# A fused attention and two-layer mixture-of-experts kernel: token gates turned earlier, sums of squares on GpSimd, router parts spread

## The chip, the cores and the metric

The kernel runs on one core of a Trainium2 chip. The metric is device time in microseconds (us), the median of several runs. Engines: TensorE (PE), VectorE (DVE), ScalarE (ACT), GpSimd (POOL), and SyncE (SP), which here only issues DMAs.

## What is computed

Sigmoid attention over 4 batches of 448 tokens, then two mixture-of-experts layers over all 1792 tokens of width 768, with 8 experts of 1024 hidden features each. Everything is fp32.

```python
def _moe2_ref(x, expert_emb, tau, w1, w2):
    xn = x / (np.linalg.norm(x, axis=-1, keepdims=True) + 1e-06)
    en = expert_emb / (np.linalg.norm(expert_emb, axis=-1, keepdims=True) + 1e-06)
    logits = xn @ en.T / tau
    expert_idx = np.argmax(logits, axis=1)
    ...
    gate_w = probs[np.arange(N), expert_idx]
    for e in range(E):
        mask = expert_idx == e
        h = np.maximum(x[mask] @ w1[e], 0.0)
        out[mask] = gate_w[mask, None] * (h @ w2[e])
```

Layer 1 (`_moe_ref`) is of the same form, with a linear router, a skip test, and `x + y` as its result. The change lies in layer 2 and in the sum of squares that its router's norm needs.

## The kernel before

**Layout.** `xT` holds x transposed: 128 features on the partitions, 6 chunks of features (`ND`), 1792 tokens along the row. A batch is 448 columns.

**A dense block.** Almost all tokens of a batch go to one expert, so that expert runs over the whole batch (`dense`, L801 on) and the few other tokens are handled by an `Item` of up to 64 tokens. Each fp32 factor is split in a high and a low part (ScalarE writes `h`, `hh`, `xs`; VectorE writes the remainders `l`, `hl`), and every product is three matmuls (L795 to L797). For f in 0 to 7 a block computes `h(f)`: 18 matmuls from `xs` into one of two PSUM banks, evicted by ScalarE (`hh`, L815) and then VectorE (`hl`, L816); and `y(f - 1)`: 18 matmuls from `hh`, `hl` into six PSUM tiles `YS`. The order on TensorE is h(0), h(1), y(0), h(2), y(1), ..., h(7), y(6), y(7).

**Sub-steps.** Other work is hung between these groups by a table of numbers: `sub(2f)` is called after h(f), `sub(2f + 1)` after y(f - 1). So sub-step 6 lies between h(3) and y(2), and 14 between h(7) and y(6). At each even sub-step the weights of the next unit are split first (`units2`, L785 and L786), then come the steps of the table. Every engine runs its own instructions in this program order.

**Banks.** `bank()` hands out the two banks in turn to whoever asks: h(f), and each small product of a router, of a gate or of an item. An item's `places` (L942) flips the turn once more, and so gets the bank that was handed out last. A matmul into a bank waits until the earlier contents have been read.

**Blocks of layer 2.** Batches j = 0, 1, 2 are stored by `finish`: VectorE transposes `YS` (L1347), GpSimd multiplies by the tokens' gates `gt` (L1349), and SP issues the stores at sub-step 2 of the next block. `gate_tokens` (L1328) makes `gt` at sub-step 14: four small VectorE operations (L357 to L361, L1333), one matmul pair (L1338), a copy (L1340). Batch 3 ends by `finish_last`, with an `Item` whose `places`, gather and gate come at sub-steps 5, 5 and 7; the gather is 64 GpSimd copies (L954) that feed L977 at sub-step 13.

**Routers of layer 2.** For batches 1 to 3 the table `ROUTED` gives the sub-steps of eight parts: raw copy and squares (ScalarE, L1075 and L1081), `squares_sum` (L1084), s1 (L245 matmuls, the last of them with the sum `G`), s2 (L262 transposes, then VectorE up to the one-hot `OH`, L283), s3 (L288, L289, then a VectorE chain), `scaled_logits`, and `gates` (L340 to L348: two ScalarE operations, then five of VectorE). Batches 1 and 2 are routed in block 0, batch 3 in block 1, batch 0 in layer 1.

Of the kernel before, what the change touches and what calls it, by code (L numbers as in the profile page):

```python
# [10 lines left out]
F32 = mybir.dt.float32  # L11
# [3 lines left out]
ALU = mybir.AluOpType  # L15
AX = mybir.AxisListType
# [5 lines left out]
def sigmoid_attention_moe_moe_kernel(  # L22
# [15 lines left out]
    nc = tc.nc  # L38
# [3 lines left out]
    P = 112  # L42
    C = S // P
    NP = H // 2
    ND = DM // 128
# [3 lines left out]
    NK = S // 32  # L49
# [8 lines left out]
    sm = ctx.enter_context(tc.tile_pool(name="sm", bufs=2))  # L58
# [7 lines left out]
    def bank(name):  # L66
        if not BANKS:
            return psA.tile([128, 512], F32, tag="psA", name=name)
        turn[0] ^= 1
        return BANKS[turn[0]]  # L70

    def spare():
        turn[1] ^= 1
        return XG[turn[1]]
# [13 lines left out]
    K = {}  # L88
# [263 lines left out]
    def dense_gate(R, b, g=None):  # L352
        t = sm.tile([P, C, NE], F32, tag="dgt", name="dgt")
        if g is None:
            g = sm.tile([P, C], F32, tag="dg", name="dg")
        one = lambda x, pat: x.rearrange(pat)
        nc.vector.tensor_mul(  # L357
            t, one(R.OH[:, ds(b, 1)], "p o e c -> p (o c) e"), R.PRIM[:P, ds(b, 1)].to_broadcast([P, C, NE])
        )
        nc.vector.reduce_sum(g, t, axis=AX.X)  # L360
        nc.vector.tensor_mul(g, g, one(K["gr"][R.m][:, ds(b, 1), :, 0], "p o c -> p (o c)"))  # L361
        return g
# [147 lines left out]
    def merge(*steps):  # L510

        out = {}
        for t in steps:
            for k in sorted(t):
                f = t[k]
                out.setdefault(k, []).extend(f if isinstance(f, list) else [f])
        return out

    def schedule(at, prep, slots):

        assert len(slots) == len(prep)
        return merge(at, *({k: f} for k, f in zip(slots, prep)))
# [164 lines left out]
    R1, R2 = Route(0), Route(1)  # L687
# [80 lines left out]
    SEL = wp.tile([128, 4 * 128], F32, tag="sel", name="sel")  # L768
# [76 lines left out]
    def at_subs(ks, fs):  # L845
        return merge(*({k: f} for k, f in zip(ks, fs)))
# [36 lines left out]
    class Item:  # L883
# [139 lines left out]
        def ready(self, k0):  # L1023

            prep = [self.places, self.gather(0, TL), self.gate]
            at = merge({k0: [self.regs, self.select]}, {5: [lambda: self.first(0)]}, {
                7: [lambda: self.first(1)], 9: [lambda: self.first(2)], 11: [lambda: self.first(3)],
                13: [self.h(0)], 14: [self.hT(0), lambda: self.second(0, 1)],
                15: [self.h(1), lambda: self.second(2, 3)],
            })  # L1030
            return at, prep
# [41 lines left out]
    def raw(b):  # L1073
        for p in range(ND):
            nc.scalar.activation(XR[:, p], batch_cols(p, b), AF.Copy)  # L1075

    SQ = ROW[:, : ND * S].rearrange("p (c s) -> p c s", s=S)
# [3 lines left out]
            nc.scalar.activation(SQ[:, p], XR[:, p], AF.Square)  # L1081

    def squares_sum():
        nc.vector.reduce_sum(K["G"], SQ.rearrange("p c s -> p s c"), axis=AX.X)  # L1084

    def batch_of(j):
        return nc.values_load(K["pb"][0:1, 8 + j : 9 + j], engines=XENG, min_val=0, max_val=B - 1)

    def expert_of(j):
        return nc.values_load(R2.I[0:1, j : j + 1], engines=[ENG.SP], min_val=0, max_val=NE - 1)  # L1090

    def route2_steps(j, xs):

        box = {}

        def halves(p):
            def f():
                if p == 0:
                    box["b"] = batch_of(j)
                    box["p"] = split_batch(xs, box["b"])  # L1100
                for g in box["p"][p : p + 2]:
                    g()

            return f

        return (
            [halves(p) for p in range(0, ND, 2)]
            + [lambda: raw(batch_of(j)), squares, squares_sum]
            + route_stages(R2, j, lambda c: XR[:, c])
            + [scaled_logits, lambda: gates(R2, j, j + 1)()]  # L1110
        )
# [8 lines left out]
    def next_dense(j):  # L1120

        box = {}
        xs = XST[(j + 1) % 2]

        def start():
            box["b"], box["e"] = rest_regs(j)
            load1(w1, box["e"], 0)
            load2(w2, box["e"], 0)
            gate_cols(R1, box["b"])

        def rows():
            gate_rows(bank("ps_G"))
            box["p"] = split_gated(xs, box["b"])
            for p in range(2):
                box["p"](p)

        def last():
            load_unit(w1, w2, box["e"], 1)
            for f in split_unit(0)[:3]:
                f()  # L1140

        return {
            8: start, 10: rows, 11: lambda: [box["p"](p) for p in (2, 3)], 12: lambda: [box["p"](p) for p in (4, 5, 6)], 13: last,
            14: lambda: [f() for f in split_unit(0)[3:]],
        }
# [115 lines left out]
    def item_steps(R, at):  # L1261
        return at_subs(at, item_list(R))
# [21 lines left out]
    with tc.If(na > 0) as cmp:  # L1284
# [4 lines left out]
        with tc.If(NB["n"] > 0) as cmp2:  # L1289
            steps = merge(next_dense(0), item_steps(R1, (10, 12, 15)), {12: lambda: raw(batch_of(0)), 15: squares})  # L1290
# [4 lines left out]
        with cmp2.Else():  # L1295
            steps = merge(rest2(), item_steps(R1, (9, 11, 12)))
# [30 lines left out]

    def gate_tokens(j, box):  # L1328

        g = dense_gate(R2, j)  # L1330
        a = spare()[:P, :128]
        four = [P, 4, C, 8]
        nc.vector.tensor_tensor(  # L1333
            a.rearrange("p (g c r) -> p g c r", g=4, r=8), g.unsqueeze(1).unsqueeze(3).to_broadcast(four),
            K["seg"][:P].unsqueeze(1).unsqueeze(1).to_broadcast(four), op=ALU.mult,
        )
        ps = bank("ps_gt")
        nc.tensor.matmul(ps[:, :NK], lhsT=a, rhs=K["off"][:P], start=True, stop=True)  # L1338
        t = box["gt"] = sm.tile([128, NK], F32, tag="gtt", name="gtt", bufs=1)
        nc.vector.tensor_copy(t, ps[:, :NK])  # L1340

    def finish(j, b, gt):

# [18 lines left out]
    def finish_last(j, b, it=None):  # L1362
# [56 lines left out]

    pend, STORES = None, []  # L1420
    ROUTED = {
        0: [(1, (1, 2, 2, 5, 6, 8, 9, 10)), (2, (7, 7, 9, 11, 12, 13, 15, 15))],
        1: [(3, (3, 7, 7, 9, 10, 11, 13, 15))],
    }
    assert B == 4
    for j in range(B):
        box = {"e": e}
        last = j == B - 1
        if last:
            todo = {}  # L1430
        else:
            todo = at_subs((3, 5, 7), route2_steps(j + 1, XST[(j + 1) % 2])[:3])
            for n, at in ROUTED.get(j, ()):
                todo = merge(todo, at_subs(at, route2_steps(n, None)[3:]))
            todo = merge(todo, {14: lambda j=j, box=box: gate_tokens(j, box)})
        if j == 0:
            load_unit(v1, v2, e, 1)
            halves()
            for f in split_unit(0, FIRST_RAW)[3:]:
                f()  # L1440
            todo = merge({-0.5: lambda: spread(item_b())}, todo)
        if j == B - 2:
            todo = merge(todo, item_steps(R2, (9, 11, 13)))
        if pend:
            todo = merge({2: pend}, todo)

        def units2(k):
            u, r = k // 4, k % 4
            if r == 0 and u + 2 < NU:
                load_unit(v1, v2, box["e"], u + 2)  # L1450
            if k == 10 and not last:
                box["n"] = expert_of(j + 1)
                load_unit(v1, v2, box["n"], 0)
            if (u + 1 < NU or not last) and r % 2 == 0:
                for f in split_unit((u + 1) % NU)[:3] if r == 0 else split_unit((u + 1) % NU)[3:]:
                    f()
            if k == 12 and not last:
                load_unit(v1, v2, box["n"], 1)

        xs = XST[j % 2]  # L1460
        if not last:
            dense(xs, beside(units2, todo))
            pend = finish(j, b, box["gt"])
            b, e = nc.values_load(K["pb"][0:1, 9 + j : 10 + j], engines=[ENG.SP], min_val=0, max_val=B - 1), box["n"]
            continue
        with tc.If(count(R2) > 0) as cmp:
            it = Item(1, 0)
            at, prep = it.ready(0)
            steps = schedule(merge(todo, at), prep, (5, 5, 7))
            dense(xs, beside(units2, steps), end=finish_last(j, b, it))  # L1470
            it.finish([None] * 3)
            info = mybir.DependencyInfo(mybir.DependencyClass.Sync, mybir.DependencyReason.DATA)
            tc.add_manual_dep(it.put().ins, STORES[0].ins.name, info, reason="the rows it lands on")
        with cmp.Else():
            STORES = []
            dense(xs, beside(units2, todo), end=finish_last(j, b))
# [36 lines left out]
```

## Time and profile before

| | |
|---|---|
| median of 3 runs | 586.06 us (585.79 to 587.38) |
| the profiled execution's own time | 585.59 us |
| its span | 583.7 us |
| busy: PE, DVE, ACT, POOL | 554.8, 303.8, 251.7, 60.5 us |
| mean granted TensorE clock | 0.984 |
| layer 2, blocks 0 to 3 start at | 290.4, 365.2, 433.5, 501.2 us |

A row of the timeline gives start, duration, engine, line, operation, output and input by name, and in brackets the idle time before it and what ended it. Matmuls are pipelined and their ends are modelled: within a run of them one starts every 0.20 us though each is shown with 0.36 us.

### The profile page before, as it was taken

The page shows a single profiled execution, that of the slowest core. Times are in us where ns is not written, and L with a number is a line of the kernel's source. Part 1 is how long each engine was busy: PE and PEld are TensorE (multiplying, and loading weights), DVE is VectorE, ACT ScalarE, POOL GpSimd, SP SyncE. Part 2 cuts the span into 40 slices and gives each one's busy share as a digit, 9 for nine tenths or more (in the row PEclk, how much of TensorE's full clock was granted, in tenths as well). Part 3 has the DMA queues.
Part 4 walks back from the last instruction along what each step waited for, and adds up shares of the span by engine and source line. Part 5 has one row for each costly group of instructions (what it writes and reads, how often), then busy time and mean ns, then how long its engine had stood idle before and what let it go on. Part 6 is the DMA issues. An engine that isn't in the chain of part 4 may idle for free.

```text
span 583.7 us, 10179 instructions
## 1 busy us (share of the span) xinstructions
PE 554.8 (95%) x3653; PEld 432.7 (74%) x3653; DVE 303.8 (52%) x775; ACT 251.7 (43%) x408; POOL 60.5 (10%) x165
## 2 busy tenths in 40 slices
PE   8999999999999999999899987999799997999995
PEld 5564645444698988998598876997789996989782
DVE  2725333456775796742288776456646432533221
ACT  5766766767722643322185511563205321222120
POOL 4010000000000001640000001200030000315300
PEclk9999999999999999999999997999989997999999
DMA  9877685746414133335470251382215633274163
GB/s 172 148 125 122 113 140 105 125 83 233 156 62 163 57 111 111 108 116 211 149 267 23 96 175 54 67 237 69 103 55 104 207 109 108 39 189 139 54 217 102
DMA packets 169261, 73.35 MB, mean 126 GB/s; under 512 B 134466, under 2 KB 160854, under 8 KB 169184
## 3 DMA queue, kind: packets, MB, share of 16 engines
q1 hardware_dynamic: 147440, 65.71, 42.0%
q10 hardware_dynamic: 21360, 6.20, 4.5%
q0 software_dynamic: 384, 0.53, 0.5%
q8 instruction: 35, 0.57, 0.4%
q14 instruction: 42, 0.34, 0.2%
HBM read 66.90 MB, written 5.70 MB: 124 GB/s over the span
## 4 chain that ended last, share of the span: by engine, by line
PE 78%; DVE 7%; issue 5%; ACT 5%; POOLq 3%; POOL 0%; DVEq 0%; ACTq 0%
PE psS L612 10%; PE psO L630 10%; PE bank L795 9%; PE y L795 8%; PE bank L797 8%; PE bank L796 8%; PE y L796 8%; PE y L797 8%; DVE l L786 2%; POOLq L952 2%; PE bank L977 2%; PE y L1001 2%; ACT h L785 1%; ACT A L616 1%; DVE G L1084 1%
## 5 line engine op out<-in xcount | busy, mean ns | idle before, releaser
L815 ACT ACTIVATE hh<-bank 128x448 fp32r<-128x448 f32 x48 | 26.2, 545 | 218.1 <-PE bank L797 174.0
L795 PE MATMUL y<-hh,h 128*128 128x448 f32 x288 | 109.8, 381 | 0.0
L795 PE MATMUL bank<-xs,h 128*128 128x448 f32 x288 | 107.1, 372 | 1.4 <-issue 0.5
L796 PE MATMUL y<-hl,h 128*128 128x448 f32 x288 | 107.8, 374 | 0.0
L797 PE MATMUL y<-hh,l 128*128 128x448 f32 x288 | 107.5, 373 | 0.0
L797 PE MATMUL bank<-xs,l 128*128 128x448 f32 x288 | 105.4, 366 | 0.1
L796 PE MATMUL bank<-xs,h 128*128 128x448 f32 x288 | 105.3, 366 | 0.0
L816 DVE SCALAR_TENSOR_TENSOR hl<-bank,hh 128x448 fp32r<-128x448 f32 x48 | 29.9, 624 | 132.3 <-ACT hh L815 131.2
L616 ACT ACTIVATE A<-psS,bias 128x896 f32<-128x896 f32 x84 | 83.3, 1006 | 34.7 <-PE psS L612 34.5
L612 PE MATMUL psS<-qT,kT 64*64 64x448 f32 x672 | 87.4, 541 | 0.4 <-ACT A L616 0.3
L786 DVE TENSOR_TENSOR l<-r,h 128x512 fp32r<-128x512 f32 (+1 forms) x115 | 85.4, 792 | 3.8 <-ACT h L785 2.0
L630 PE MATMUL psO<-A,v 64*64 64x448 f32 x672 | 86.4, 539 | 0.0
L785 ACT ACTIVATE h<-r 128x512 fp32r<-128x512 f32 (+1 forms) x115 | 74.4, 708 | 0.0
L795 PEld LDWEIGHTS bank<-xs,h 128*128 128x128 f32 x288 | 54.1, 188 | 9.8 <-issue 2.5
L795 PEld LDWEIGHTS y<-hh,h 128*128 128x128 f32 x288 | 55.9, 194 | 5.9 <-issue 1.0
L797 PEld LDWEIGHTS y<-hh,l 128*128 128x128 f32 x288 | 55.8, 194 | 4.8
L796 PEld LDWEIGHTS y<-hl,h 128*128 128x128 f32 x288 | 55.9, 194 | 4.6 <-issue 0.2
L630 PEld LDWEIGHTS psO<-A,v 64*64 64x64 f32 x672 | 34.7, 133 | 32.3 <-issue 20.0
L797 PEld LDWEIGHTS bank<-xs,l 128*128 128x128 f32 x288 | 54.1, 188 | 5.0 <-DVE l L786 0.4
L796 PEld LDWEIGHTS bank<-xs,h 128*128 128x128 f32 x288 | 54.1, 188 | 4.2
L612 PEld LDWEIGHTS psS<-qT,kT 64*64 64x64 f32 x672 | 32.4, 132 | 30.5 <-issue 16.2
L954 POOL COPY row<-xT 128x6 f32 x64 | 18.2, 305 | 210.5 <-PE bank L795 198.3
(264 smaller groups left out, 441.7 us busy)
## 6 DMA issues: line engine op xcount, KB each, us to landing
r<-in_moe_w_dram SPq DMA_DIRECT2D x62, 768.0 KB, 4.6
k<-in_k_dram SPq DMA_DIRECT2D x44, 112.0 KB, 2.9
q<-in_q_dram SPq DMA_DIRECT2D x44, 112.0 KB, 3.3
v<-in_v_dram ACTq DMA_DIRECT2D x44, 112.0 KB, 2.8
out_dram<-row SPq DMA_DIRECT2D x12, 336.0 KB, 3.8
stg<-in_moe_w_dram SPq DMA_DIRECT2D x1, 768.0 KB, 6.6
row<-in_moe_w_dram SPq DMA_DIRECT2D x1, 768.0 KB, 8.3
out_dram<-row SPq DMA_DIRECT2D x1, 672.0 KB, 4.0
```

What stands on the lines that cost most here:

```text
L612: nc.tensor.matmul(ps[KT * i : KT * i + KT, j, :S], lhsT=kT[r, i, h * KT : (h + 1) * KT], rhs=qT[r, i], start=True, stop=True,)
L616: nc.scalar.activation(at, ps[:, :, :S], AF.Sigmoid, bias=bias, scale=1.0 / math.sqrt(D))
L630: nc.tensor.matmul(ST[w, "o"][i][D * j : D * j + D, :S], lhsT=t[r, j, h, :], rhs=at[r, j, :], start=h == 0, stop=h == NH - 1,)
L785: nc.scalar.activation(dst_h, src, AF.Copy)
L786: nc.vector.tensor_sub(dst_l, src, dst_h.bitcast(F32))
L795: nc.tensor.matmul(ps, lhsT=ah, rhs=bh, start=first, stop=False)
L796: nc.tensor.matmul(ps, lhsT=ah, rhs=bl, start=False, stop=False)
L797: nc.tensor.matmul(ps, lhsT=al, rhs=bh, start=False, stop=last)
L815: nc.scalar.activation(a, ps[:, :S], AF.Relu)
L816: nc.vector.scalar_tensor_tensor(l, ps[:, :S], 0.0, a.bitcast(F32), op0=ALU.max, op1=ALU.subtract)
L952: o = nc.values_load(self.places_[0:1, t : t + 1], engines=[ENG.Pool], min_val=0, max_val=NT - 1, skip_runtime_bounds_check_because="place ...
L954: nc.gpsimd.tensor_copy(self.xb[:, :, t : t + 1], xT[:, :, ds(o, 1)])
```

## The change

```diff
 def squares_sum():
-    nc.vector.reduce_sum(K["G"], SQ.rearrange("p c s -> p s c"), axis=AX.X)
+    for p in range(1, ND):
+        nc.gpsimd.tensor_tensor(K["G"], K["G"] if p > 1 else SQ[:, 0], SQ[:, p], op=ALU.add)
 ...
 def gate_tokens(j, box):
-    g = dense_gate(R2, j)
-    a = spare()[:P, :128]
-    four = [P, 4, C, 8]
-    nc.vector.tensor_tensor(
-        a.rearrange("p (g c r) -> p g c r", g=4, r=8), g.unsqueeze(1).unsqueeze(3).to_broadcast(four),
-        K["seg"][:P].unsqueeze(1).unsqueeze(1).to_broadcast(four), op=ALU.mult,
-    )
-    ps = bank("ps_gt")
-    nc.tensor.matmul(ps[:, :NK], lhsT=a, rhs=K["off"][:P], start=True, stop=True)
-    t = box["gt"] = sm.tile([128, NK], F32, tag="gtt", name="gtt", bufs=1)
-    nc.vector.tensor_copy(t, ps[:, :NK])
+    a = SEL[:P, :128]
+    def ready():
+        g = dense_gate(R2, j)
+        four = [P, 4, C, 8]
+        nc.vector.tensor_tensor(
+            a.rearrange("p (g c r) -> p g c r", g=4, r=8), g.unsqueeze(1).unsqueeze(3).to_broadcast(four),
+            K["seg"][:P].unsqueeze(1).unsqueeze(1).to_broadcast(four), op=ALU.mult,
+        )
+    def turned():
+        ps = bank("ps_gt")
+        nc.tensor.matmul(ps[:, :NK], lhsT=a, rhs=K["off"][:P], start=True, stop=True)
+        t = box["gt"] = sm.tile([128, NK], F32, tag="gtt", name="gtt", bufs=1)
+        nc.vector.tensor_copy(t, ps[:, :NK])
+    return {3: ready, 6: turned}
 ...
 ROUTED = {
-    0: [(1, (1, 2, 2, 5, 6, 8, 9, 10)), (2, (7, 7, 9, 11, 12, 13, 15, 15))],
-    1: [(3, (3, 7, 7, 9, 10, 11, 13, 15))],
+    0: [(1, (1, 2, 2, 5, 6, 8, 9, 9)), (2, (7, 8, 8, 11, 12, 14, 15, 15))],
+    1: [(3, (3, 7, 7, 9, 10, 12, 13, 15))],
 }
 ...
-    todo = merge(todo, {14: lambda j=j, box=box: gate_tokens(j, box)})
+    todo = merge(todo, gate_tokens(j, box))
 ...
-    steps = schedule(merge(todo, at), prep, (5, 5, 7))
+    steps = schedule(merge(todo, at), prep, (4, 4, 7))
```

The VectorE half of `gate_tokens` now stands at sub-step 3, its TensorE half at 6, and its matrix lies in `SEL` instead of a spare tile. `squares_sum` is five additions in a chain on GpSimd, in place of one VectorE reduction; it is called four times in the executed path. In block 0 the squares and the sum of batch 2 stand at sub-step 8 (7 and 9 before), its s3 at 14 (13 before), and the gates of batch 1 at 9 (10 before). In block 1 the s3 of batch 3 stands at 12 (11 before). The last block's `places` and gather stand at sub-step 4. In the changed file L1338 is L1343.

**Sub-step 14 of block 0, on TensorE.** Before: the last matmuls of h(7), into bank 0, then the gate, then y(6).

```order
L796 MATMUL bank0_1729<-xs0_93,h11_1741 128x448
L797 MATMUL bank0_1729<-xs0_93,l11_1742 128x448
L1338 MATMUL bank1_1730<-off_372,xg1_74 128x14
L795 MATMUL y0_1731<-hh0_75,h21_1743 128x448
L796 MATMUL y0_1731<-hl0_77,h21_1743 128x448
```

Now:

```order
L796 MATMUL bank0_1729<-xs0_93,h11_1741 128x448
L797 MATMUL bank0_1729<-xs0_93,l11_1742 128x448
L288 MATMUL bank1_1730<-OH1_106,tri_317 128x32
L289 MATMUL bank1_1730<-OH1_106,one_321 128x32
L795 MATMUL y0_1731<-hh0_75,h21_1743 128x448
```

The gate is gone from there, and s3 of batch 2 has come in its place; in blocks 1 and 2 y(6) follows h(7) at once.

**Sub-step 6 of block 0, on TensorE.** The end of h(3), into bank 1, then the transposes of s2 of batch 1, and in the changed kernel the gate.

```order
L796 MATMUL bank1_1730<-xs0_93,h11_1741 128x448
L797 MATMUL bank1_1730<-xs0_93,l11_1742 128x448
L262 MATMUL bank0_1729<-ident_81,xg1_74 112x128 x2
L1343 MATMUL bank1_1730<-off_372,sel_1748 128x14
L795 MATMUL y0_1731<-hh0_75,h21_1743 128x448
L796 MATMUL y0_1731<-hl0_77,h21_1743 128x448
```

The gate writes bank 1, which h(3) has just filled. In blocks 1 and 2 no other product stands between, and the gate there writes bank 0, while h(3) is in bank 1.

**Sub-step 4 of the last block, on TensorE, in the changed kernel.** The end of h(2), `places`, and y(1).

```order
L796 MATMUL bank1_1730<-xs1_94,h11_1741 128x448
L797 MATMUL bank1_1730<-xs1_94,l11_1742 128x448
L942 MATMUL bank1_1730<-sel_1748,small_1749 1x64 x4
L795 MATMUL y0_1731<-hh1_76,h20_1739 128x448
L796 MATMUL y0_1731<-hl1_78,h20_1739 128x448
```

Before, y(1) stood between h(2) and `places`, which wrote bank 1 as well.

## Rows read from the trace of the kernel before

**Rows 1.** The page, part 1: busy time, share of the span, instructions.

```profile
PE 554.8 (95%) x3653; PEld 432.7 (74%) x3653; DVE 303.8 (52%) x775; ACT 251.7 (43%) x408; POOL 60.5 (10%) x165
```

**Rows 2.** Who waited for whom, TensorE: us in total, times, longest.

```profile
PE bank L1338 <- DVE xg L1333: 12.4, 3, 4.1
...
PE bank L288 <- DVE OH L283: 1.4, 2, 0.8
...
PE bank L977 <- POOL stg L954: 1.0, 1, 1.0
```

**Rows 3.** Timeline at sub-step 14 of block 0: the weight splits on VectorE.

```profile
352.65 1.83 DVE L786 TENSOR_TENSOR l<-r,h 128x768 fp32r<-128x768 f32 x2
...
```

**Rows 4.** Stretches: us, PE, PEld, DVE, ACT, POOL busy (x), PEclk, DMA share, GB/s.

```profile
355.84:365.22 9.38, 9.38 (x37) 8.53 (x38) 6.90 (x28) 0.35 (x2) 1.96 (x3) 0.77 0.22 80
424.57:433.52 8.95, 8.95 (x39) 8.17 (x39) 4.01 (x11) 0.00 (x0) 1.97 (x3) 0.81 0.27 88
491.35:501.19 9.84, 9.84 (x37) 8.91 (x38) 3.01 (x6) 0.00 (x0) 2.06 (x3) 0.73 0.23 76
372.42:379.79 7.37, 7.37 (x37) 6.76 (x36) 3.52 (x5) 5.75 (x11) 0.00 (x0) 1.00 0.55 96
...
337.60:345.00 7.40, 7.40 (x45) 6.45 (x46) 5.17 (x12) 2.46 (x5) 0.00 (x0) 1.00 0.41 138
```

**Rows 5.** Timeline at sub-step 6 of block 0: y(2) starts, `hl` of h(3).

```profile
315.56 0.45 PE L795 MATMUL y<-hh,h 128*128 128x448 f32 x1
...
316.26 0.62 DVE L816 SCALAR_TENSOR_TENSOR hl<-bank,hh 128x448 fp32r<-128x448 f32 x1 [2.05 <-ACT hh L815]
```

**Rows 6.** Groups by line: out<-in xcount | busy us, mean ns | idle before.

```profile
L1084 DVE TENSOR_REDUCE G<-row 128x448 f32<-128x2688 f32 x4 | 20.0, 4988 | 2.9 <-ACT row L1081 2.9
...
L1349 POOL TENSOR_TENSOR row<-stg,gtt 128x448 f32<-128x448 f32 x18 | 16.3, 941 | 228.5 <-DVE stg L1347 228.5
...
L128 POOL TENSOR_SCALAR emb<-emb,embss 8x768 f32<-8x768 f32 x1 | 2.2, 2247 | 20.9 <-DVE embss L127 20.9
```

**Rows 7.** Timeline of block 0, sub-steps 8 to 11: squares, h(4), router chain, sum.

```profile
321.33 2.90 ACT L1081 ACTIVATE row<-stg 128x448 f32<-128x448 f32 x6
...
322.72 0.37 PE L797 MATMUL bank<-xs,l 128*128 128x448 f32 x1
...
324.56 1.66 ACT L785 ACTIVATE h<-r 128x512 fp32r<-128x512 f32 x3
...
327.04 0.22 DVE L291 COPY tt<-bank 128x64 f32<-128x64 f32 x1
...
332.57 0.19 DVE L332 TENSOR_TENSOR SH<-SH,nr 112x32 f32<-112x32 f32 x1
...
337.56 0.38 PE L245 MATMUL bank<-G,sqw 128*32 128x224 f32 x2 [2.23 <-DVE G L1084]
...
338.45 0.47 PE L795 MATMUL bank<-xs,h 128*128 128x448 f32 x1
```

**Rows 8.** Timeline of the last block's gather, GpSimd and VectorE.

```profile
525.20 0.20 POOL L954 COPY stg<-xT 128x6 f32 x1 [0.28 <-issue]
...
525.33 1.83 DVE L786 TENSOR_TENSOR l<-r,h 128x768 fp32r<-128x768 f32 x2
...
525.66 2.07 POOL L954 COPY stg<-xT 128x6 f32 x5 [0.27 <-issue]
```

**Rows 9.** Timeline at the end of block 0, VectorE: gates, transposes.

```profile
359.98 0.35 DVE L344 RECIPROCAL ge<-ge 112x32 f32<-112x32 f32 x1 [0.41 <-ACT ge L341]
...
362.38 3.69 DVE L1347 STREAM_TRANSPOSE stg<-y 128x448 f32<-128x448 f32 x6 [1.19 <-PE y L797]
```

**Rows 10.** Timeline of the last block, sub-steps 4 and 5: TensorE and VectorE.

```profile
515.79 0.37 PE L795 MATMUL y<-hh,h 128*128 128x448 f32 x1
...
516.57 0.62 DVE L816 SCALAR_TENSOR_TENSOR hl<-bank,hh 128x448 fp32r<-128x448 f32 x1 [3.66 <-ACT hh L815]
...
520.26 0.21 DVE L945 TENSOR_SCALAR stg<-bank 1x64 int32<-1x64 f32 x1 [1.26 <-PE bank L942]
```

## The prediction

> **What bounds the kernel now.** I began with the page: TensorE is busy for 554.8 of 583.7 us [rows 1], so only what delays TensorE can move the end, and at most 28.9 us of idle time is there to be had. The second view is who waited for whom, for TensorE alone [rows 2]. Its longest entry is the tokens' gate: L1338 waited three times for VectorE's L1333, 12.4 us in all and at most 4.1. Two more entries end on things that the change moves, s3 waiting for the one-hot (1.4 us) and the item's first product waiting for the gather (1.0 us). One further wait is in the timeline: the last part of s1 of batch 2 waited 2.23 us for the reduction L1084 [rows 7].
>
> The timeline shows why the gate waits. At sub-step 14 TensorE ends h(7), and the next thing in its queue is the gate. VectorE has first to evict h(7) and to split weights until 354.48 (352.65 + 1.83, [rows 3]), and only then comes to the gate's four operations. y(6), which stands behind the gate, needs none of this.
>
> The third view is the table of stretches [rows 4], which holds what the listing of waits hides. The 36 matmuls of y(6) and y(7) behind each gate took 9.38, 8.95 and 9.84 us at a granted clock of 0.77, 0.81 and 0.73, so part of the time at the lower level, 1.2 GHz. 36 such matmuls at full clock (2.4 GHz) took 7.37 us. In each of the three cases the fall follows the wait of 4.1 us; behind the wait of 2.23 us the clock stayed at 1.00 (the last of [rows 4]).
>
> **The change, part by part.** All sums are made against the profiled execution's own 585.59 us.
>
> *The gate leaves sub-step 14.* The wait goes: 12.4 us. What comes next in TensorE's queue is y(6), whose factors were evicted one group earlier; y(7) needs the `hl` of h(7), which VectorE has 1.3 us after h(7) ends (as for h(3): 316.88 in [rows 5], against its end near 315.58), while y(6) lasts 3.7 us. So nothing is late there next. In block 0, s3 now stands at this place; it needs `OH`, made a whole group earlier.
>
> *The clock.* With no long wait ahead of them, the three stretches should take 7.37 us each: (9.38 + 8.95 + 9.84) - 3 x 7.37 = 6.1 us [rows 4]. Ends: 0 if the clock falls all the same, 6.1 if it stays up.
>
> *The reduction moves to GpSimd.* TensorE's 2.23 us go if the sum is ready when s1 reaches its last part, which would be at 337.56 - 2.23 = 335.33 [rows 7]. The squares now stand behind the split that ended at 324.56 + 1.66 = 326.22 and take 2.90, so the second is there by 327.2 and the last by 329.1. No row shows a chained GpSimd addition of this size. The nearest is GpSimd's multiply of the same 128x448 with two inputs, 0.94 us; a slower bound is L128, 2.25 us for 768 elements, or 1.31 us for 448 [rows 6]. I take 0.94, as it has the same shape: five in a row end at 331.9, at the bound at 333.8, both ahead of 335.33. VectorE loses four operations of 4.99 us, GpSimd gains 20 of 0.94; no other TensorE wait ended on L1084. Nothing of GpSimd's is held up: its next work is the multiply at the block's end.
>
> *s3 one group later* (sub-steps 13 to 14, 11 to 12): both waits go, 1.4 us.
>
> *One correction.* A listed wait counts from the modelled end of the matmul before, some 0.36 us after its start (0.37 in [rows 7]), while in a run the next starts 0.20 after it (7.37 / 36, [rows 4]). Each of the seven waits therefore holds 0.16 us more: 1.1 us.
>
> *places at sub-step 4.* The gather starts when L945 has run, at 520.26 before [rows 10]. In its new place L945 follows `hl` and three splits (517.19 + 1.9, so 519.1), over 1 us earlier, and TensorE reaches L977 later by the new wait below. The 1.0 us of that wait go; it was GpSimd that released it, not a load of weights [rows 2].
>
> Gains: 12.4 + 6.1 + 2.2 + 1.4 + 1.0 + 1.1 = **24.2 us**.
>
> **What it adds.** Two new waits, both on a bank.
>
> - In block 0 the gate at sub-step 6 writes bank 1, just filled by h(3). It must wait until VectorE has read it: 316.26 + 0.62 = 316.88, where y(2) started at 315.56 [rows 5]. That is 1.3 us, and y(2) stands behind it. In blocks 1 and 2 the gate gets the other bank and waits for nothing. The matmul pair itself costs the same at either place.
> - In the last block, `places` writes the bank of h(2) directly behind it: 516.57 + 0.62 - 515.79 = 1.4 us [rows 10]. Before, y(1) lay in between.
>
> Next, batch 1's gates (9 instead of 10) put ScalarE's `ge` ahead of the eviction of h(5). It waits for VectorE's chain L291 to L332, 332.76 - 327.04 = 5.7 us [rows 7], which starts some 0.8 us earlier than before, as the squares no longer delay the eviction of h(4). Then come 0.41 for `ge`, 1.2 for the gates (359.98 to 362.38 - 1.19, [rows 9]), and 0.62 for `hl` [rows 5]: 334.2 against 338.45 - 2.23 = 336.2, when h(6) wants that bank. A margin of 2.0 us, so nothing by itself.
>
> But the additions and this chain now run side by side. The two engines do get in each other's way [rows 8]: GpSimd's 128x6 copies take 0.20 us alone, yet 2.07 for five while VectorE subtracts two SBUF tiles. VectorE's subtractions took 1.83 us with GpSimd active and 1.83 without [rows 3, 8], but those copies are short. If each addition held VectorE for its whole 0.94 us, the chain would be 4.7 us late and h(6) 2.7; if VectorE keeps going, 0. I take half the hold, 2.4 - 2.0 = 0.4 us.
>
> The Trainium skill bears on this: SBUF — State Buffer, section Who interferes with whom, says that a VectorE instruction with two SBUF inputs contends with a GpSimd instruction that reads SBUF, and that whichever issues first keeps the port for the whole instruction. The trace agrees for GpSimd's copies (2.07 us for five); no row shows VectorE held. By that rule the upper of the two ends, 2.7 us, would stand in the sum instead of 0.4.
>
> Last, the end of block 0. From h(7)'s end VectorE has `hl` (1.3, as above) and two splits (1.83, [rows 3]), now s3's chain and the scaled logits (5.7), 0.41, the gates (1.2), the transposes (3.69, [rows 9]) and `hl` of h(0) (0.62): +14.8. TensorE needs that `hl` after s3 (0.4), y(6), y(7) (7.4) and h(0), h(1) (7.2, from 365.22 to 372.42, [rows 4]): +15.0 and its first matmul. I take 0.1 us, with ends 0 and 1. GpSimd's multiplies and SP's stores start 6 us later against h(0) than before; the loads that queue behind them on SP feed h(6) of block 1, four groups after their split, which covers it.
>
> Losses: 1.3 + 1.4 + 0.4 + 0.1 = **3.2 us**. Net gain 21.0 us: 564.6 us for an execution like the profiled one, which lay 0.5 us below the median of 586.06. **Predicted median: 565.1 us.**
>
> **Rivals.**
>
> 1. *GpSimd holds VectorE* for all five additions: 2.3 us more, and 1 more at block 0's end: 568.4. For it: the stretched copies [rows 8]. Against: VectorE's durations did not move there. Chance 0.15.
> 2. *The bank waits and the hold cost nothing*, because evictions are quicker or y fills in: 561.9. Against: TensorE runs in order, and the evictions are timed in [rows 5, 10]. Chance 0.1.
> 3. *The clock does not come back*: some low stretches remain, set off by the new waits of 1.3 and 1.4 us: up to 571.2. Against: 2.23 us did not do it. Chance 0.08.
> 4. *Slower than before*: chained additions far dearer than 0.94 us, so that TensorE waits at all four s1 products. To lose 21.0 + 1.8 us takes 5.7 at each; with the 3.4 us of cover seen in block 0 (335.33 - 331.9), a sum must take 4.7 + 9.1 = 13.8 us, 2.8 per addition, over twice the slower bound. It decides from there; just beyond, 588. Chance 0.02.
>
> **How the numbers follow.** The sum as it stands has 0.65. A measurement of this kernel can tell about 0.3% (1.8 us) from no change. All cases but the fourth end far below that line, so faster 0.96, same 0.02 (a sum near 2.6 us per addition), slower 0.02. The range reaches from rival 2 to beyond rival 1, with part of rival 3: 561.9 to 569.5.
>
> **What would show it.** Right: no entry of TensorE on the gate's VectorE operation; 7.4 us for y(6) and y(7) at a granted clock of 1.00; no wait on the sum; two new entries, the gate in block 0 and `places` in the last block, of 1.2 to 1.4 us, both released by `hl` (L816); L1084's successor at about 0.94 us per addition. Wrong: a wait of h(6) in block 0 on `hl`, VectorE's small operations stretched beside the additions, a clock below 1.00 between 300 and 550 us, or a wait of y(0) at the start of block 1.

## The result, and the profile after

The changed kernel took **565.56 us** in the median of 4 executions (564.89 to 568.04), the kernel before 586.43 us beside it: a ratio of 0.965, with a 95% interval of 0.962 to 0.968. The forecast was 565.1 us. The profiled execution took 565.9 us (before: 585.59), with a span of 564.1 us, so 19.7 us went where the working said 21.0.

The page, part 1, as in [rows 1]:

```profile
PE 547.1 (97%) x3653; PEld 426.9 (76%) x3653; DVE 294.3 (52%) x771; ACT 251.6 (45%) x408; POOL 85.9 (15%) x185
```

TensorE is busy for 97% of the span instead of 95%. VectorE lost 9.5 us and not the 20 of the four reductions, GpSimd gained 25.4 us and not 18.8. The dearer additions, and 4.5 us of VectorE's difference, are told below; the rest of VectorE's lies in other operations that ran beside GpSimd's work, the weight splits (L786) above all, 88.6 us in place of 85.4.

Who waited for whom, TensorE (us in total, times, longest), against [rows 2]:

```profile
PE bank L795 <- DVE hl L816: 2.5, 2, 2.4
...
PE bank L942 <- DVE hl L816: 1.3, 1, 1.3
PE bank L1343 <- DVE hl L816: 1.1, 1, 1.1
```

The 12.4 us of the gate, the waits for `OH` and the gather, and that for the sum are gone. L942 and L1343 are the two bank waits that were expected, of about their size. The first entry is one that the sum had at 0.4 us: it is h(6) of block 0, with 2.37 us.

The stretches of y(6) and y(7) of blocks 0, 1 and 2, in the columns of [rows 4]:

```profile
352.21:359.59 7.38, 7.38 (x38) 6.85 (x38) 6.24 (x29) 1.84 (x3) 0.00 (x0) 1.00 0.34 108
413.38:420.67 7.29, 7.29 (x37) 6.76 (x36) 6.98 (x19) 2.25 (x5) 2.05 (x3) 1.00 0.37 107
473.68:480.99 7.31, 7.31 (x37) 6.77 (x37) 5.29 (x8) 2.01 (x3) 2.05 (x3) 1.00 0.54 178
```

They take 21.98 us together, against 28.17 in the first three of [rows 4], and the granted clock is 1.00 in each: 6.2 us, where 6.1 were forecast.

The timeline of block 0 around VectorE's chain of batch 1, the part that [rows 7] showed of before:

```profile
328.27 0.22 DVE L291 COPY tt<-bank 128x64 f32<-128x64 f32 x1
328.52 0.17 DVE L294 TENSOR_TENSOR tt<-tt 128x8 f32<-128x8 f32 x1
328.61 1.16 DVE L296 TENSOR_TENSOR tt<-tt 128x8 f32<-128x8 f32 x1
329.80 0.17 DVE L294 TENSOR_TENSOR tt<-tt 128x8 f32<-128x8 f32 x1
...
332.53 0.99 DVE L304 SCALAR_TENSOR_TENSOR d<-CNT,RF,desc 128x8 f32<-128x8 f32 x1
333.56 0.16 DVE L307 TENSOR_REDUCE RF<-d 128x1 f32<-128x8 f32 x1
333.75 1.00 DVE L308 TENSOR_SCALAR PRIM<-d,RF 128x8 f32<-128x8 f32 x1
...
338.24 0.19 DVE L332 TENSOR_TENSOR SH<-SH,nr 112x32 f32<-112x32 f32 x1
338.84 0.35 DVE L344 RECIPROCAL ge<-ge 112x32 f32<-112x32 f32 x1 [0.41 <-ACT ge L341]
...
339.98 0.59 DVE L816 SCALAR_TENSOR_TENSOR hl<-bank,hh 128x448 fp32r<-128x448 f32 x1
...
328.51 1.22 POOL L1085 TENSOR_TENSOR G<-row 128x448 f32<-128x448 f32 x1 [18.42 <-ACT row L1081]
329.81 4.91 POOL L1085 TENSOR_TENSOR G<-G,row 128x448 f32<-128x448 f32 x4
...
340.62 0.47 PE L795 MATMUL bank<-xs,h 128*128 128x448 f32 x1 [2.37 <-DVE hl L816]
```

While GpSimd adds (328.51 to 334.72), five VectorE operations on 128x8, which the kernel below without most of the additions shows at 0.17 and 0.23 us, last about 1 us each: L296 three times, L304 and L308. The reduction L307 between them is not stretched. Nor is L294, which has two SBUF inputs like L296 but starts in the gap before an addition (at 329.80, the addition at 329.81). The chain from L291 to L332 takes 338.43 - 328.27 = 10.2 us instead of 5.7. Behind it in VectorE's queue stand the gates and then `hl` of h(5), whose bank h(6) wants.

The additions, by line:

```profile
L1085 POOL TENSOR_TENSOR G<-G,row 128x448 f32<-128x448 f32 x16 | 19.4, 1214 | 1.3
...
L1085 POOL TENSOR_TENSOR G<-row 128x448 f32<-128x448 f32 x4 | 5.1, 1277 | 254.8 <-ACT row L1081 238.4
```

They take 1.21 to 1.28 us each in the mean, not 0.94, near the 1.31 that was the slower bound. No product waited for the sum.

Longer operations of VectorE are held as well. Three splits of 128x512 took, in the kernel before:

```profile
325.24 1.89 DVE L786 TENSOR_TENSOR l<-r,h 128x512 fp32r<-128x512 f32 x3
```

and in the changed kernel, beside the additions of batch 3 (387.17 to 392.36):

```profile
390.36 3.14 DVE L786 TENSOR_TENSOR l<-r,h 128x512 fp32r<-128x512 f32 x3
```

No product waited for these.

### The profile page after: what moved, and what is told of

It reads as the page before. It is cut to its first block, busy times and chain, and to the rows that moved or that the text cites. A ratio compares the mean times of both kernels' runs of the same rounds, so it can differ in the third digit from the quotient of the medians.

```text
span 564.1 us, 10214 instructions
## 1 busy us (share of the span) xinstructions
PE 547.1 (97%) x3653; PEld 426.9 (76%) x3653; DVE 294.3 (52%) x771; ACT 251.6 (45%) x408; POOL 85.9 (15%) x185
## 4 chain that ended last, share of the span: by engine, by line
PE 83%; DVE 7%; issue 3%; ACT 2%; DMA 2%; SPq 1%; DVEq 1%; POOL 0%; POOLq 0%; ACTq 0%
PE y L795 10%; PE bank L795 10%; PE y L796 10%; PE y L797 10%; PE bank L797 9%; PE bank L796 9%; PE psO L630 9%; PE psS L612 9%; PE bank L977 2%; PE y L1001 2%; DMA q<-in_q_dram 1%; DVE l L786 1%; ACT A L616 1%; SPq L565 1%; PE ps_r L245 1%
## 5 line engine op out<-in xcount | busy, mean ns | idle before, releaser
L795 PE MATMUL y<-hh,h 128*128 128x448 f32 x288 | 107.4, 373 | 0.0
L797 PE MATMUL y<-hh,l 128*128 128x448 f32 x288 | 105.3, 366 | 0.0
L796 PE MATMUL y<-hl,h 128*128 128x448 f32 x288 | 105.3, 365 | 0.0
L786 DVE TENSOR_TENSOR l<-r,h 128x512 fp32r<-128x512 f32 (+1 forms) x115 | 88.6, 820 | 3.6 <-ACT h L785 2.0
L795 PEld LDWEIGHTS y<-hh,h 128*128 128x128 f32 x288 | 54.1, 188 | 5.7 <-issue 1.0
L797 PEld LDWEIGHTS y<-hh,l 128*128 128x128 f32 x288 | 54.1, 188 | 4.5
L796 PEld LDWEIGHTS y<-hl,h 128*128 128x128 f32 x288 | 54.1, 188 | 4.3 <-issue 0.2
L1085 POOL TENSOR_TENSOR G<-row 128x448 f32<-128x448 f32 x4 | 5.1, 1277 | 254.8 <-ACT row L1081 238.4
```

The costliest lines, as they stand in the source:

```text
L786: nc.vector.tensor_sub(dst_l, src, dst_h.bitcast(F32))
L795: nc.tensor.matmul(ps, lhsT=ah, rhs=bh, start=first, stop=False)
L796: nc.tensor.matmul(ps, lhsT=ah, rhs=bl, start=False, stop=False)
L797: nc.tensor.matmul(ps, lhsT=al, rhs=bh, start=False, stop=last)
```

## The experiments

All are built on the changed kernel; each is compared with the kernel before on the same chip (586.5 to 587.1 us there).

**1. The logits and gates of batch 1 later, and the gates alone.**

```diff
-        0: [(1, (1, 2, 2, 5, 6, 8, 9, 9)), (2, (7, 8, 8, 11, 12, 14, 15, 15))],
+        0: [(1, (1, 2, 2, 5, 6, 8, 10, 10)), (2, (7, 8, 8, 11, 12, 14, 15, 15))],
```

> The scaled logits and the gates of batch 1 go from sub-step 9 to 10, so that VectorE evicts h(5) of block 0 as soon as the chain up to L319 is done (335.07 in the trace of the changed kernel) and not behind the square roots and the gates. Theory (the 2.37 us wait of h(6) is the held chain, with the gates queued ahead of hl): hl ends before h(6) wants its bank at 338.26, the wait goes, 565.6 - 2.4 = 163.2 + 400 = 563.2 us, ratio to before 0.961. Rival (the gates' place is not what matters, ScalarE's eviction is late): the wait stays over 1.5 us, 565 us or more.

The second kernel has (1, 2, 2, 5, 6, 8, 9, 10) at the same place.

> Only the gates of batch 1 go back to sub-step 10, the scaled logits stay at 9: this part of the change is undone. Theory (the additions held the chain by 4.4 us, the gates' place added the rest): hl of h(5) runs right behind L332, 338.43 + 0.62 = 339.05, so the wait of h(6) shrinks from 2.37 to about 0.8 us: 565.6 - 1.6 = 564.0 us. Rival (the gates' place alone made the wait, the hold is harmless): the wait goes, 563.2 us.

Measured: 563.39 us (ratio 0.959, interval 0.958 to 0.961) and 565.12 us (0.963, 0.962 to 0.964). The start of the chain and `hl` of h(5) in the first:

```profile
328.82 1.20 DVE L294 TENSOR_TENSOR tt<-tt 128x8 f32<-128x8 f32 x1
329.94 0.16 DVE L296 TENSOR_TENSOR tt<-tt 128x8 f32<-128x8 f32 x1
...
335.23 0.62 DVE L816 SCALAR_TENSOR_TENSOR hl<-bank,hh 128x448 fp32r<-128x448 f32 x1
```

and in the second, with the product that waits for it:

```profile
338.11 0.19 DVE L332 TENSOR_TENSOR SH<-SH,nr 112x32 f32<-112x32 f32 x1
338.22 0.62 DVE L816 SCALAR_TENSOR_TENSOR hl<-bank,hh 128x448 fp32r<-128x448 f32 x1
...
338.90 0.47 PE L795 MATMUL bank<-xs,h 128*128 128x448 f32 x1 [0.71 <-DVE hl L816]
```

In the first the wait is gone, in the second 0.71 us of it is left (0.8 expected). The chain is held in the first as well, but there L294 lasts 1.20 us and L296 behind it 0.16: which of the two is held goes by their starts against those of the additions (the first addition starts at 328.82 there too). So the whole wait has two parts: the held chain, which alone leaves 0.71 us, and the gates queued ahead of `hl`. The traces decide this; the second run's time, 1.1 us above its expectation, does not.

**2. One addition instead of five.** The kernel leaves out four of the five additions of the sum of squares, so norms and gate weights differ.

```diff
-        for p in range(1, ND):
-            nc.gpsimd.tensor_tensor(K["G"], K["G"] if p > 1 else SQ[:, 0], SQ[:, p], op=ALU.add)
+        nc.gpsimd.tensor_tensor(K["G"], SQ[:, 0], SQ[:, 5], op=ALU.add)
```

> Leaves four of the five additions of the sum of squares out, so the norm and with it the gate weights are others; all else is as in the changed kernel. Theory (GpSimd's five additions hold VectorE's chain by 4.4 us, some 0.9 each): one hold of 0.8 to 1.0 us is left, the chain from L291 to L332 takes 5.7 + 1 = 6.7 us, hl of h(5) is there at about 336.6, before h(6) wants its bank, the wait of 2.37 goes: 563.2 us. Rival (the chain is long because of the order of the gates and of the eviction, not of GpSimd): the chain keeps its 10 us or the wait stays over 1.5 us, 565 us or more.

Measured: 562.99 us (0.960, 0.958 to 0.962). Timeline of the same place:

```profile
327.93 0.17 DVE L296 TENSOR_TENSOR tt<-tt 128x8 f32<-128x8 f32 x1
...
328.93 0.23 DVE L304 SCALAR_TENSOR_TENSOR d<-CNT,RF,desc 128x8 f32<-128x8 f32 x1
...
329.38 0.23 DVE L308 TENSOR_SCALAR PRIM<-d,RF 128x8 f32<-128x8 f32 x1
...
329.77 1.12 DVE L319 SCALAR_TENSOR_TENSOR CE<-PRIM,CNT 128x8 f32<-128x8 f32 x1
...
334.07 0.19 DVE L332 TENSOR_TENSOR SH<-SH,nr 112x32 f32<-112x32 f32 x1
...
335.81 0.59 DVE L816 SCALAR_TENSOR_TENSOR hl<-bank,hh 128x448 fp32r<-128x448 f32 x1
...
329.70 1.17 POOL L1084 TENSOR_TENSOR G<-row 128x448 f32<-128x448 f32 x1 [24.04 <-ACT row L1081]
```

The one addition, which waits for the last square, starts behind the five operations that had been held, and they are back at 0.17 and 0.23 us. It holds one other, as expected: L319, with two SBUF tiles, lasts until the addition ends (329.77 + 1.12 = 330.89, against 329.70 + 1.17 = 330.87). In the changed kernel L319 ran behind the last addition, in 0.16 us. So the chain takes 334.26 - 327.59 = 6.7 us, one hold more than before the change, and h(6) does not wait. The order of the gates is that of the changed kernel, so the additions beside these operations are shown as the cause of the stretching, one operation for each addition.

**3. The sum back on VectorE.**

```diff
+        nc.vector.reduce_sum(K["G"], SQ.rearrange("p c s -> p s c"), axis=AX.X)
...
+        0: [(1, (1, 2, 2, 5, 6, 8, 9, 10)), (2, (7, 7, 9, 11, 12, 14, 15, 15))],
```

> The sum of squares is VectorE's reduction again, and the parts of block 0 that were moved for it (squares and sum of batch 2 at sub-steps 7 and 9, gates of batch 1 at 10) stand where they stood; the gate, s3 and places stay as changed. Theory (the move to GpSimd gave back what it won): the wait of h(6) for hl goes (2.4 us) and s1 waits 2.2 us for the sum again, 565.4 us, no difference to the changed kernel, and no VectorE operation of 128x8 over 0.3 us. Rival (the move was worth its 2.2 us by itself): 567.8 us.

Measured: 564.91 us (0.963, 0.961 to 0.965). Timeline:

```profile
333.75 4.93 DVE L1084 TENSOR_REDUCE G<-row 128x448 f32<-128x2688 f32 x1
338.59 0.62 DVE L816 SCALAR_TENSOR_TENSOR hl<-bank,hh 128x448 fp32r<-128x448 f32 x1
...
338.73 0.38 PE L245 MATMUL bank<-G,sqw 128*32 128x224 f32 x2 [1.32 <-DVE G L1084]
```

s1 waits for the sum again, 1.32 us rather than 2.2, and h(6) no longer waits. The move to GpSimd was worth nothing here: by the waits it cost 1 us (2.37 at `hl` in place of 1.32 for the sum), and the two times, 564.91 and 565.56 us, do not differ beyond their intervals.

**4. The two bank waits, one at a time.** The gate's TensorE half one sub-step later; in another kernel, `places` of layer 2 into the other bank.

```diff
-        return {3: ready, 6: turned}
+        return {3: ready, 7: turned}
```

> The TensorE half of the gate one sub-step later, at 7, where h(3) has long been evicted. Theory (the 1.13 us at L1343 in block 0 is the bank of h(3)): it goes, in the other blocks nothing changes, 565.6 - 1.1 - 0.1 = 564.4 us. Rival (any small product between two groups costs its wait, whatever its bank): a wait of about 1 us stands at the new place, 565.6 us.

```diff
-            turn[0] ^= 1
+            turn[0] ^= self.m == 0
             ps = bank("ps_pl")
+            turn[0] ^= self.m
```

> In layer 2 alone, places writes the bank that h(2) has not just filled (the turn is flipped behind the call, not ahead of it). Theory (the 1.29 us at L942 in the last block is the wait for hl of h(2) on that bank, and nothing else): the wait goes, 565.6 - 1.3 - 0.1 = 564.2 us, less up to 0.3 if h(3), which now shares the bank, waits for VectorE's copy of the places. Rival (the gather's start sets the item's end, so the time comes back at L977): no change, 565.6.

Measured: 565.66 us (0.964, 0.963 to 0.966) and 566.58 us (0.965, 0.963 to 0.967): no gain to be seen in either time, although in both traces the wait aimed at is gone and none has come in its place. The table of stretches tells why. In the 5 us behind the wait of h(6), the first run's trace has

```profile
339.00:344.00 5.00, 4.96 (x17) 4.47 (x18) 1.72 (x2) 0.37 (x2) 0.00 (x0) 0.66 1.04 368
```

and the second's

```profile
340.00:345.00 5.00, 4.99 (x17) 4.52 (x18) 1.69 (x2) 0.34 (x2) 0.00 (x0) 0.66 1.04 361
```

with 17 matmuls, where the changed kernel's profiled execution started 26 at a clock of 1.00:

```profile
340.60:345.60 5.00, 4.98 (x26) 4.62 (x27) 2.12 (x3) 1.35 (x5) 0.00 (x0) 1.00 1.04 363
```

A clock of 0.66 for 5 us loses 1.7 us. So here the wait of 2.3 us was followed by a fall to 1.2 GHz for part of the time, and the gain of 1.3 or 1.4 us drowned in it. Without that 1.7 us the two profiled executions, of 566.23 and 565.87 us, would have taken 564.5 and 564.2, as expected; this is worked out, not measured. The forecast's rival on the clock looked at the waits of 1.3 and 1.4 us for this; it is the wait of h(6) that does it. The next run checks that the changed kernel itself has it both ways.

**5. The changed kernel again.** No edit.

> The changed kernel once more, beside the two that follow. Theory (its wait of h(6) of 2.37 us is followed by a fall of the clock in some executions and not in others): about 565.6 us, with executions spread over some 2 us and the longer ones at the lower mean clock. Rival (the clock does not matter here): all executions within 0.5 us.

Measured: 567.29 us (0.966, 0.964 to 0.969), executions of 565.67 to 568.00. The profiled one, 568.0 us:

```profile
338.90:341.20 2.30, 0.01 (x1) 0.00 (x1) 1.75 (x8) 2.16 (x6) 0.00 (x0) 1.00 0.98 341
341.20:346.20 5.00, 5.00 (x17) 4.51 (x18) 1.68 (x2) 0.33 (x2) 0.00 (x0) 0.66 1.04 368
```

Over both measurements, the five executions with a mean clock of 0.998 or 0.999 took 564.89 to 566.45 us, the four with 0.994 or 0.995 took 567.29 to 568.04. So the change's own time has two values, some 2 us apart, and a median says how many of each there were; that of all nine is 566.45 us. Only two of the nine have a trace, and for the others the mean clock is all that tells them apart.

**6. The whole gate at the end of h(7) again, ahead of the splits and behind them.**

```diff
-        return {3: ready, 6: turned}
+        return {13.5: [ready, turned]}
```

> The whole gate at the end of h(7) again, but ahead of the two splits on VectorE: the wait lasts 4.1 - 1.83 = 2.3 us in place of 4.1. Theory (what counts is the length of each wait; one of 2.2 us left the clock at 1.00 in the kernel before, while the 2.36 and 2.29 us of two other runs were followed by 0.58 to 0.83): three waits of 2.3 us, 565.6 + 3 x (2.3 + 0.16) - 1.2 = 571.8 us with no fall, and up to 1.7 more for each fall: 571.8 to 576.9 us, some of the three stretches at 1.00 and some lower. Rival (any wait for the gate at this place drops the clock as far as one of 4.1 us did): three stretches of 9 us or more, 571.8 + 6.1 = 577.9 us or above.

Behind the splits it is `{14: [ready, turned]}`.

> Both halves of the gate back at sub-step 14 behind the splits; the sum on GpSimd, the table and the early places stay. Theory (the gate's place is 12.4 us of waits plus 6.1 us of clock): L1343 waits three times some 4 us, the stretches of y(6) and y(7) behind them take 9 us or more each at a granted clock of 0.7 to 0.8, the bank wait of block 0 (1.1 + 0.1) is gone: 565.6 + 12.4 + 0.5 + 6.1 - 1.2 = 583.4 us. Rival (the clock fell for another reason, say the reduction's wait ahead of it): waits return, the stretches take 7.4 us each: 577.3 us.

Measured: 576.08 us (0.982, 0.980 to 0.984) and 588.65 us (1.002, 1.000 to 1.004). Stretches of the first: the 5 us behind the wait of h(6), and behind the gate of blocks 0, 1 and 2.

```profile
339.00:344.00 5.00, 5.00 (x17) 4.49 (x18) 1.66 (x2) 0.32 (x2) 0.00 (x0) 0.66 1.05 368
...
354.10:359.10 5.00, 4.99 (x27) 4.69 (x28) 4.25 (x21) 0.00 (x0) 0.00 (x0) 1.00 0.28 70
...
418.40:423.40 5.00, 4.99 (x25) 4.65 (x26) 3.13 (x9) 0.00 (x0) 0.00 (x0) 1.00 0.29 67
...
481.30:486.30 5.00, 5.00 (x18) 4.50 (x19) 1.93 (x3) 0.00 (x0) 0.00 (x0) 0.66 0.26 41
```

The waits ahead of them were 2.30, 2.15, 2.40 and 2.15 us. Two were followed by a fall and two were not, with no order by their length. The sum holds: 565.9 + 6.7 (the gate's three waits) + 0.5 - 1.2 + 2 x 1.7 = 575.3 us, against 575.72 for the profiled execution.

The second, the kernel before as far as the gate goes, is 5 us above what was expected. Its waits and one row of its timeline:

```profile
PE bank L1343 <- DVE sel L1336: 14.2, 3, 6.0
```

```profile
357.44 0.60 PE L1343 MATMUL bank<-off,sel 112*128 112x14 f32 x2 [5.98 <-DVE sel L1336]
```

In block 0 s3 of batch 2 now also stands at 14, and its chain ran on VectorE ahead of the gate: 5.98 us instead of some 4. The 9 us behind each gate were at a granted clock of 0.68, 0.69 and 0.63:

```profile
357.40:366.40 9.00, 8.96 (x32) 8.13 (x33) 5.58 (x26) 0.35 (x2) 0.74 (x1) 0.68 0.08 32
...
425.90:434.90 9.00, 8.95 (x32) 8.14 (x33) 2.78 (x9) 0.00 (x0) 0.84 (x1) 0.69 0.30 89
...
493.20:502.20 9.00, 8.95 (x30) 8.10 (x31) 1.35 (x3) 0.00 (x0) 0.39 (x1) 0.63 0.28 87
```

That is 9.0 x (0.32 + 0.31 + 0.37) = 9.0 us rather than some 6, and the wait of h(6) (2.23 us in this run) was followed by a fall as well. Summed: 565.9 + 14.2 + 0.5 - 1.2 + 9.0 + 1.7 = 590.1 us for an execution of 589.03. So the gate's place with what follows it carries the change's gain: with the gate back, and the longer wait that s3 gives it here, nothing is left of it.

**7. All three waits taken away; and the same with the sum on VectorE.** The edits of 1 (first run) and 4 together; in the second kernel that of 3 as well, with the squares and the sum of batch 2 at 7 and 9.

> Logits and gates of batch 1 at sub-step 10, the TensorE half of the gate at 7, places of layer 2 into the other bank: the three waits that the change added are all taken away. Theory (each was on the path, and no other wait is behind them): against the kernel with the logits at 10 alone (563.4 us) the waits of 1.1 and 1.3 us and 0.1 each for the modelled ends go: 560.8 us, all stretches between 290 and 500 us at a granted clock of 1.00. Rival (the waits only stand in for others, as the two runs with one of them removed suggested): 562.5 us or more.

> The same with the sum of squares as VectorE's reduction, and the squares and sum of batch 2 at sub-steps 7 and 9 as before the change. Theory (with the logits behind it the reduction runs from some 330.5 to 335.5 and is there before s1 asks for it at 337, so GpSimd's additions are worth nothing): the same time as the run beside it, within 0.5 us. Rival (taking 20 us off VectorE pays somewhere): 1 us or more slower, with a wait for G or for an eviction to show for it.

Measured: **561.03 us** (0.956, 0.954 to 0.959) and 562.40 us (0.959, 0.957 to 0.961). TensorE's longest waits in the first:

```profile
PE busy L648 <- POOL ident masks.py:199: 1.3, 1, 1.3
PE y L1002 <- DVE xT L1175: 1.0, 1, 1.0
PE bank L795 <- ACT xs L862: 0.8, 1, 0.8
```

Nothing in layer 2 waits for `hl` any more, and the granted clock is 1.00 in every stretch from 290 to 540 us. This version beats both kernels, the changed one by 4.5 us or more. The second run's reduction on VectorE:

```profile
330.25 5.04 DVE L1085 TENSOR_REDUCE G<-row 128x448 f32<-128x2688 f32 x1
335.19 0.63 DVE L816 SCALAR_TENSOR_TENSOR hl<-bank,hh 128x448 fp32r<-128x448 f32 x1
```

It ends ahead of s1, and no product waits for it. The two profiled executions took 562.33 and 561.91 us; the medians lie 1.4 us apart the other way, with overlapping intervals. Whether GpSimd's additions are worth anything once nothing waits stays open; no row shows a gain.

## Why the prediction was right, and where it was not

- *The gate leaves sub-step 14 (12.4 us) and the clock (6.1 us)*: right, 12.4 and 6.2 in the trace. The second kernel of run 6 returns both by putting the gate back, and more than both (14.2 and 9.0 us), because s3 stands ahead of the gate there.
- *The sum (2.2), s3 (1.4), the gather (1.0)*: right, none of the three waits is left. That s3 and the gather gained is read from the trace; no run undoes either alone. The price of an addition was too low, 0.94 us for 1.21 to 1.28; the cover of 3.4 us that the text counted took it, as the bound of 1.31 had said.
- *The two bank waits (1.3 and 1.4 us)*: right, 1.13 and 1.29 listed, 0.16 more each by the correction. Runs 4 and 7 show the bank as the cause. By these rows the early `places` cost more than it gained (1.45 us at its bank, 1.12 at the gather, each with its 0.16): as it stands, this part of the change is a small loss.
- *The end of block 0 (0.1 us)*: nothing. `hl` of h(0) was there at 366.14, y(0) of block 1 started at 366.79.
- *The additions beside VectorE's chain*: **this is the step that failed**: "I take half the hold, 2.4 - 2.0 = 0.4 us". Its margin of 2.0 us was right: 338.26, when h(6) asked, less 328.27 + 5.7 + 0.41 + 1.2 + 0.62 gives 2.1. The mechanism was right too; that only half of it would come rested on no row. The hold was 4.4 us and not 2.4, so the term measured 2.37, and two of the text's own signs of being wrong are there, the wait of h(6) and the stretched operations. That is the first rival, priced at 2.7 us in block 0; its other half, 1 us at the block's end, did not come. The full hold follows from the row: each addition held one operation until it ended, so five operations that need 0.17 to 0.23 us gained 4.5 us. The splits that the text set against it ("VectorE's durations did not move there") do move beside the longer additions, from 1.89 to 3.14 us for three. The sentence cited from the Trainium skill, SBUF — State Buffer, section Who interferes with whom, had the upper end, and the trace agrees with it: L296 with two SBUF inputs lasts 1.16 us beside an addition and 0.17 without, and the reduction L307 0.16 beside one.
- *The clock does not come back*: partly so, at another place than the third rival said. The text's "2.23 us did not do it" rested on a single case; in these runs waits of 2.15 to 2.40 us went either way.
- *The net*: 24.3 us of gains and 1.3 + 1.5 + 2.5 of losses (each with its 0.16) are 19.0 us, the profiled execution shows 19.7. The two best-measured terms carry most of it. That the median came within 0.5 us of the forecast is in part luck: the profiled execution missed its 564.6 us by 1.3, but it lay 0.3 us above its median where the text had put it 0.5 below, and the median was taken over executions most of which kept the clock. The 567.29 us of the second measurement is 2.2 us above the forecast, and within the range.

## What to carry to other kernels

An operation that TensorE needs only later should not stand in its queue behind a busy VectorE: here three waits of 4 us cost 12.4 us and the clock behind them another 6. Before work is moved to GpSimd, look at which VectorE operations will run beside it: here a short one on two SBUF tiles that started during an addition lasted until the addition ended, about 1 us in place of 0.2, and what counts is whose eviction is queued behind it. When one removed wait shows no gain, read the granted clock behind the waits that are left before calling the removal worthless.

## What was not expected of the hardware

- A GpSimd addition in a chain on 128x448 fp32 took 1.21 us, and 1.17 us when it was the only one; GpSimd's multiply with the tokens' gates took 0.94 us before [rows 6].
- L308, a TENSOR_SCALAR with one 128x8 tile and a column of scalars as inputs, was held to 1.00 us like those with two tiles.
- After waits of TensorE of 2.15 to 2.40 us the granted clock fell in some cases (2.15, 2.23, 2.29 twice, 2.30, 2.36 us) and stayed at 1.00 in others (2.15, 2.37, 2.40 us, and the 2.23 of the kernel before). After the waits of 1.3 us and less that this text names it stayed at 1.00, after all those of 4 us and more it fell. What else decides it the runs do not show.
